# A long-convolution and MLP kernel: two filter blocks transformed whole, a wide-matmul FIR, DMA transposes for five MLP inputs, folded inverses, a new order

## The chip, the cores and the metric

The kernel runs on one core of a Trainium2 chip. TensorE multiplies matrices and writes to PSUM, VectorE and ScalarE do element-wise work, GpSimd computes the small powers of the norms and issues accumulating DMAs, and SyncE issues the other DMAs. The metric is the device time in microseconds (us); a time without a label is the median of several runs. Times inside a profile are those of one profiled execution, counted from the start of its span.

## The reference, cut to what matters

The input is one sequence of 2048 positions with 512 channels in bf16. It passes twice through two layers:

```python
x = A_q
x = x + A(layernorm(x), A_k, A_v, shift_k, ssm_k, ssm_D)
x = x + B(layernorm(x), w1, b1, w2, b2)
x = x + A(layernorm(x), A_k, A_v, shift_k, ssm_k, ssm_D)
x = x + B(layernorm(x), w1, b1, w2, b2)
```

Layer A shifts k with a causal FIR filter of four taps per channel (`shift_k`), multiplies by v to get kv, convolves kv along the positions with a causal filter as long as the sequence (`ssm_k`, in the reference by FFT), adds `kv * ssm_D`, and multiplies the result y by its normalised input q. Since k and v do not depend on x, y is the same in both passes. Layer B is an MLP: a second layernorm, a matrix of 512 x 1376, GELU, a matrix of 1376 x 512, and biases.

## The kernel before, in words

**Blocks.** The sequence is cut into four blocks of 512 positions. One buffer `ar` in SBUF holds everything in bf16, `sm` the statistics, `ps` is PSUM. In a block a partition holds four neighbouring positions, so that a tile is 128 x 512 (positions by channels).

**The convolution.** Each block of kv and each block of the filter is transformed to 512 odd frequencies by matmuls with a table of cosines and sines (`forward`, line 582, for kv; `spectrum_h`, line 598, for the filter, which first transposes it on TensorE). `forward` uses a symmetry: the even and the odd positions are transformed apart (two matmuls for each of two outputs, four tiles, 16 matmuls of 512 columns a block, in `freq`, line 575), ScalarE evicts each tile out of PSUM, and VectorE makes the sum and the difference, which are the frequencies and their mirror images. Products of spectra of blocks j and b-j are made on VectorE (`products`, line 677), and for j over 0 are added into the accumulator by accumulating DMAs that GpSimd issues (`accumulate`, line 620). `wrap` (line 664) adds the wrapped part of the previous filter block. At the end of `products` VectorE combines real and imaginary parts and the mirrored halves; `inverse` (line 709) turns the result into y, for blocks 1 to 3 with 16 matmuls of 512 columns.

**The FIR.** `shift` (line 622) transposes k on TensorE, evicts it into a layout with one spare column for the previous block's last value, and multiplies by diagonal matrices of the four taps (built by one VectorE instruction, line 570). A half block takes 32 matmuls of 128 columns (line 648); two halves, four blocks, 256 matmuls. VectorE multiplies the result by v (block 0 straight out of PSUM, line 657).

**The MLP.** `mlp(b, L)` (line 784) does layer A's last step and layer B for block b in pass L. For two pairs of 128-position tiles it computes statistics on VectorE or ScalarE, the power on GpSimd (line 738), the last coefficient on VectorE (line 739), the norm on ScalarE (line 779), multiplies by y, adds, and does a second norm the same way. The normalised pair is transposed by eight 128 x 128 transposes on TensorE (line 807) and evicted by ScalarE or VectorE (lines 563 and 564) into the MLP's input. The first matrix follows (line 824; 44 matmuls of 512 columns, or 88 of 256 where `PARTS`, line 860, cuts the block in two), GELU on ScalarE (line 829), the second matrix (line 843; 44 of 512 columns), and VectorE adds the result to x (line 848 in pass 0, with the sum for the next mean; line 851 in pass 1).

**What sets the order.** The program is recorded as a list of operations with their reads and writes. A written-out list (`ORDER`) says in which order each engine takes its operations, `BANKS` which PSUM bank each tile has, and `SIDE` which of those that could run on ScalarE or VectorE take the second choice. Engines work strictly in this order and wait for each other by semaphores; SyncE and GpSimd issue DMAs in their order too. `keep_busy` fills TensorE's longer planned gaps with idle matmuls (line 913; 34 of them here).

**Program order around the change.** H0, block 0's convolution, H1, MLP(0,0), block 1's convolution, H2, H3, the wraps, then MLPs and the convolutions of blocks 2 and 3. The order list interleaves all of it.

Of the kernel before, what the change touches and what calls it, by code (L numbers as in the profile page):

```python
# [366 lines left out]
def _tables():  # L367

    t = np.arange(4)[:, None] + 4 * np.arange(128)[None, :]
    kk = np.arange(2)[:, None] + 2 * np.arange(128)[None, :]  # L370
    th = TWO_PI * t[:, :, None, None] * (kk + 0.5) / 1024
    F = np.stack([np.cos(th), -np.sin(th)], 3)
    return F.transpose(1, 0, 2, 3, 4).reshape(128, 2048), F.transpose(4, 2, 3, 0, 1).reshape(128, 2048) / 512


SIDE = [30, 204, 508, 590, 728, 750, 831, 912, 933]
BANKS = "020402242404224400262556463010456340262616542032024240042240042440066016553462243501654013266102613202040404062341663552015021261526103315215340424444026015654624643030521242141654360010665123404156021610322554431541243501601"
ORDER = [
# [47 lines left out]
def bass_interleave_layers__ssm_conv_h3__mixer_channel_mlp__prompt_kernel(  # L426
# [141 lines left out]
    dg = A(0, 128, R_DG, [128, 16], [1, 128])  # L568
    i3, s3 = A(0, 128, R_ID, [0, 16], [1, 128]), A(0, 128, R_S, [1, 16], [0, 128])
    P.op(DVE, lambda e: e.tensor_tensor(dg, i3, s3, ALU.mult), 2300.0, reads=[i3, s3], writes=[dg])  # L570
# [26 lines left out]

    def spectrum_h(m):
# [10 lines left out]
        if m == 0:  # L609
            tt(A(0, 1, o, [1, U]), A(0, 1, o, [1, U]), A(0, 1, R_D, [1, U]), ALU.add, 512)  # L610
        forward(o, R_H[m], (R_TMP, R_HT[0], R_EO[0], R_EO[0])[m], m > 0)
# [10 lines left out]
    def shift(b):  # L622
        kt = R_KT[b % 2]
        tl = Tile(P, 2)
        ins = [(c, i, A(0, 128, KS(b) + i * U + c * 128, [1, 128])) for c in range(4) for i in range(4)]

        def f(e, ins=ins, tl=tl):
            for c, i, src in ins:
                r = e.transpose(QB(tl, 0, 128, c * U + i * 128, [1, 128]), src, IDN)  # L629
            return r  # L630
        P.op(PE, f, 16 * 60.0, reads=[x[2] for x in ins] + [IDN], tile=tl)
        copy(A(0, 128, kt + 1, [129, 16], [1, 128]), tl, lambda tl=tl: QB(tl, 0, 128, 0, [128, 16], [1, 128]), 2048, (ACT, DVE), True)
        if b:
            d, e0 = A(0, 128, kt, [129, 16]), A(0, 128, R_KT[1 - b % 2] + 128, [129, 16])
            P.op(DVE, lambda e: e.tensor_copy(d, e0), 110.0, reads=[e0], writes=[d])
        for h in range(2):
            tl = Tile(P, 2)
            ins = []
# [237 lines left out]
    spectrum_h(0)  # L876
    conv(0)
    tag("H1")
    spectrum_h(1)
    tag("KP")  # L880
    keep()
    tag("W1")
# [61 lines left out]
```

## Time and profile before

| what | us |
|---|---|
| median of 3 runs | 246.11 (245.12 to 246.13) |
| the profiled execution's own time | 244.91 |
| its span | 243.1 |

The span is what the profile covers; its own time has 1.8 us around it. In the lists of the profile, a row names the line of the kernel, the engine, the operation, the output and input, the tile sizes and the count. `ar<-ps` is a move from PSUM to SBUF. The mean duration of a matmul in those lists is longer than the distance between two of them, since they are pipelined; distances are read from the chain of work that ended last, whose pieces follow one another without overlap. The chain gives a start, a length and a run of instructions for each piece. The table of stretches gives the busy time of each engine in chosen parts of the span.

### The profile page before, as it was taken

Reading aid. Unit: us, or ns where it says so; the run is one execution under the profiler, and the core shown is the slowest. Engines: PE = TensorE matmul, PEld = TensorE weight load, DVE = VectorE, ACT = ScalarE, POOL = GpSimd, SP = SyncE. Lnnn points to the kernel's source line nnn. Section 1 sums busy time; section 2 is a strip of 40 time slices with the busy share of each in tenths; the row PEclk is TensorE's granted clock in tenths of the full one; section 3 lists DMA queues with packets and bytes.
Section 4 is the critical chain, followed back from the end, with each engine's and each line's share of the span. In section 5 each row is a group of like instructions: output and inputs, shape, how many; then the busy total and the mean of one; then the engine's idle time right before and its main releaser. Section 6 shows DMA issues by size and latency. Waiting matters only on the chain.

```text
span 243.1 us, 3962 instructions
## 1 busy us (share of the span) xinstructions
PE 232.9 (96%) x1551; PEld 131.9 (54%) x1574; DVE 185.1 (76%) x357; ACT 181.6 (75%) x279; POOL 68.0 (28%) x73
## 2 busy tenths in 40 slices
PE   8999996989999999999999999999999999999994
PEld 3756632647655684445444544544468654448841
DVE  1379999999999999999999999783977242574004
ACT  2358998999899589979799285579968657955730
POOL 0000134432572356753146315241310201120000
PEclk9999999999999999999999999999999999999999
DMA  6999916668794099990089989920002000002002
GB/s 189 392 377 220 391 52 238 105 242 162 142 158 62 0 173 173 175 174 3 0 162 185 172 215 226 207 47 3 1 0 89 0 0 3 0 0 86 3 0 86
DMA packets 14406, 29.85 MB, mean 123 GB/s; under 512 B 3026, under 2 KB 8500, under 8 KB 14260
## 3 DMA queue, kind: packets, MB, share of 16 engines
q0 software_dynamic: 5232, 15.21, 32.9%
q1 hardware_dynamic: 9156, 14.40, 17.2%
q8 instruction: 12, 0.20, 0.3%
q14 instruction: 6, 0.05, 0.1%
HBM read 12.30 MB, written 2.10 MB: 59 GB/s over the span
## 4 chain that ended last, share of the span: by engine, by line
PE 67%; DVE 22%; issue 5%; ACT 3%; POOL 2%; DVEq 0%; POOLq 0%
PE ps L824 28%; PE ps L843 26%; DVE ar L557 14%; PE ps L575 6%; DVE sm L750 4%; PE ps L913 3%; PE ps L807 2%; POOL sm L738 2%; ACT ar L779 1%; DVE ar L657 1%; ACT ar L563 1%; DVE ar L851 1%; PE ps L629 1%; PE ps L648 1%; DVE sm L752 1%
## 5 line engine op out<-in xcount | busy, mean ns | idle before, releaser
L557 DVE TENSOR_TENSOR ar<-ar 128x2048 bf16<-128x2048 bf16 (+2 forms) x125 | 115.1, 954 | 9.3 <-ACT ar L563 4.8
L824 PE MATMUL ps<-ar 128*128 128x256 bf16 (+3 forms) x479 | 80.2, 320 | 1.2 <-ACT ar L563 0.9
L563 ACT ACTIVATE ar<-ps 128x1024 bf16<-128x1024 f32 (+2 forms) x61 | 64.3, 1115 | 22.0 <-PE ps L575 10.3
L843 PE MATMUL ps<-ar 128*128 128x512 bf16 (+1 forms) x339 | 79.6, 379 | 0.7
L829 ACT ACTIVATE ar<-ps,sm 128x256 bf16<-128x256 f32 (+3 forms) x121 | 61.5, 572 | 16.5 <-PE ps L824 16.2
L738 POOL TENSOR_TENSOR sm<-sm 128x2 f32<-128x2 f32 x32 | 39.0, 1218 | 104.6 <-DVE sm L757 45.1
L824 PEld LDWEIGHTS ps<-ar 128*128 128x128 bf16 (+1 forms) x484 | 47.7, 100 | 32.3 <-ACT ar L563 1.8
L779 ACT ACTIVATE ar<-ar,sm 128x512 bf16<-128x512 bf16 x64 | 48.4, 808 | 13.3 <-DVE sm L739 13.1
L843 PEld LDWEIGHTS ps<-ar 128*128 128x128 bf16 (+1 forms) x352 | 34.1, 98 | 37.0 <-ACT ar L829 1.2
L575 PE MATMUL ps<-ar 128*128 128x512 bf16 x187 | 44.4, 380 | 3.5 <-ACT ar L563 2.7
L620 POOL DMA_DIRECT2D ar<-ar x30 | 27.5, 931 | 44.8 <-DVE ar L557 25.3
L750 DVE BATCH_NORM_STATS2 sm<-ar 128x6 f32<-128x512 bf16 x48 | 32.5, 687 | 0.4
L575 PEld LDWEIGHTS ps<-ar 128*128 128x128 bf16 x192 | 17.2, 98 | 27.2 <-ACT ar L563 7.7
L851 DVE TENSOR_TENSOR ar<-ps,ar 128x512 bf16<-128x512 f32 x16 | 10.9, 686 | 16.6 <-PE ps L843 16.5
L848 DVE SCALAR_TENSOR_TENSOR ar<-ps,ar 128x512 bf16<-128x512 f32 x16 | 11.0, 685 | 8.4 <-PE ps L843 8.3
L648 PE MATMUL ps<-ar 128*128 128x128 bf16 x256 | 15.6, 219 | 0.3 <-ACT ar L563 0.2
L648 PEld LDWEIGHTS ps<-ar 128*128 128x128 bf16 x256 | 14.7, 98 | 1.8 <-ACT ar L563 0.7
L564 DVE COPY ar<-ps 128x1024 bf16<-128x1024 bf16 (+1 forms) x9 | 7.3, 808 | 7.7 <-PE ps L605 3.9
L771 ACT ACTIVATE ar<-ar,sm 128x512 bf16<-128x512 bf16 x16 | 11.5, 717 | 0.1
L913 PE MATMUL ps<-ar 128*128 128x512 bf16 x34 | 9.4, 428 | 1.0 <-DVE ar L523 1.0
L807 PE MATMUL ps<-ar 128*128 128x128 bf16 x128 | 9.5, 219 | 0.5 <-ACT ar L779 0.4
L807 PEld LDWEIGHTS ps<-ar 128*128 128x128 bf16 x128 | 8.1, 98 | 3.0 <-ACT ar L779 0.9
(27 smaller groups left out, 53.5 us busy)
## 6 DMA issues: line engine op xcount, KB each, us to landing
ar<-ar POOLq DMA_DIRECT2D x24, 512.0 KB, 4.9
ar<-in_A_k_dram SPq DMA_DIRECT2D x4, 512.0 KB, 5.6
ar<-in_A_ssm_k_dram SPq DMA_DIRECT2D x4, 512.0 KB, 8.0
ar<-in_A_v_dram SPq DMA_DIRECT2D x4, 512.0 KB, 5.8
ar<-in_A_q_dram SPq DMA_DIRECT2D x4, 512.0 KB, 7.0
ar<-ar POOLq DMA_DIRECT2D x6, 256.0 KB, 4.6
out_dram<-ar SPq DMA_DIRECT2D x3, 512.0 KB, 2.6
ar<-in_B_w_dram SPq DMA_DIRECT2D x1, 1376.0 KB, 7.1
```

The costliest lines, as they stand in the source:

```text
L557: return P.op(DVE, lambda e: e.tensor_tensor(o, a, b, op), 66.0 + 0.52 * n, reads=[a, b], writes=[o])
L563: return e.activation(dst, src(), AF.Copy)
L575: r = e.matmul(Q(tl, 0, 128, ri * 512, [1, 512]), w, m, start=a, stop=z)
L620: P.op(POOL, lambda e: e.dma_start(dst, src, accum_op=ALU.add), 880.0, reads=[src, dst], writes=[dst], dma=True, nbytes=nb)
L648: r = e.matmul(Q(tl, 0, 128, q, [1, 128]), w, m, start=j == 0, stop=j == 3)
L738: P.op(POOL, lambda e: e.tensor_tensor(r, v, hf, ALU.pow), 1100.0, reads=[v, hf], writes=[r])
L750: P.op(DVE, lambda e, st=st, x=x: e.bn_stats(st, x), 600.0, reads=[x], writes=[st])
L779: P.op(ACT, lambda e: e.activation(o, x, AF.Identity, bias=m, scale=r), 705.0, reads=[x, m, r], writes=[o])
L807: r = e.transpose(QB(tl, 0, 128, 256 * j + 128 * a, [1, 128]), src[4 * a + j], IDN)
L824: r = e.matmul(Q(tl, 0, rows, 0, [1, n]), w, m, start=dk == 0, stop=dk == 3)
L829: P.op(ACT, lambda e, dst=dst, tl=tl, rows=rows, bias=bias, n=n: e.activation(dst, Q(tl, 0, rows, 0, [1, n]), AF.Gelu_apprx_tanh, bias=bia ...
L843: r = e.matmul(Q(tl, 0, 128, 0, [1, 512]), ins[fc][0], ins[fc][1], start=fc == 0, stop=fc == 10)
```

## The change

1. **Filter blocks 1 and 2 transformed whole.** A new `direct` replaces `forward` for them: for each of the four outputs all eight matmuls (four positions, real and imaginary) accumulate in one PSUM tile, 32 matmuls a block instead of 16, and the sum and difference on VectorE go. A negated copy of half of the table (`negate`, one instruction, on ScalarE by `SIDE`) supplies the mirrored outputs.
2. **Frequency numbering.** The second half of the frequencies is numbered from the other end (`768 * np.arange(2)`), which makes the two halves mirror images in the time fold; `wrap` treats both halves alike (a subtraction on VectorE, an accumulation by DMA).
3. **FIR in wide matmuls.** For a channel group seven matmuls of 512, 384, 256, 128, 384, 256 and 128 columns replace sixteen of 128; 112 in all instead of 256, over the same number of columns. The diagonals are built in two halves, and block 0's transposes and evictions are cut in two.
4. **Five MLP inputs transposed by DMA.** For MLPs (1,1), (2,0), (2,1), (3,0) and (3,1) SyncE issues four DMA transposes of 128 x 512 each (20 in all, 128 KB each) straight from the normalised tile into the MLP's input; their 80 transposes on TensorE and ten evictions go.
5. **Inverses of blocks 2 and 3 folded once more.** Four more VectorE products of 1024 elements at the end of `products` halve the inverse: 8 matmuls instead of 16.
6. **H2 is recorded ahead of MLP(0,0)**, the power's planned cost falls from 1100 to 690 ns, and `ORDER`, `BANKS` and `SIDE` are new. By the new order the idle matmuls are 28.

```diff
-    kk = np.arange(2)[:, None] + 2 * np.arange(128)[None, :]
+    kk = 768 * np.arange(2)[:, None] + 2 * np.arange(128)[None, :]
...
-SIDE = [30, 204, 508, 590, 728, 750, 831, 912, 933]
+SIDE = [32, 216]
...
+    negf = A(0, 128, R_HT[0] + 4096, [512, 2], [1, 512])
+    posf = A(0, 128, R_F + 512, [1024, 2], [1, 512])
...
+    P.op((ACT, DVE), negate, {ACT: 930.0, DVE: 360.0}, reads=[posf], writes=[negf])
+
+    def direct(src, dst):
+
+        for c in range(2):
+            for z in range(2):
+                tl = Tile(P, 2)
+                ins = []
+                for ri in range(2):
+                    for i in range(4):
+                        w = A(0, 128, R_HT[0] + 4096 + ((i // 2 * 2 + c) * 2 + ri) * 128, [1, 128]) if z and i % 2 else fw(i, c, ri)
+                        ins.append((ri, i == 0, i == 3, w, A(0, 128, src + i * U, [1, U])))
+                freq(tl, ins)
+                copy(A(0, 128, dst + 2 * c * 1024 + z * 1024, [1, 1024]), tl, lambda tl=tl: Q(tl, 0, 128, 0, [1, 1024]), 1024)
...
+        if m in (1, 2):
+            return direct(o, R_H[m])
...
             for z in range(2):
-                i = 2 * h + z
-                for c in range(4):
-                    for j in range(4):
-                        ins.append((z * 512 + c * 128, j, A(0, 128, kt + (c * 4 + (i - j) % 4) * 129 + (i >= j), [1, 128]),
-                                    A(0, 128, R_DG + (c * 4 + j) * 128, [1, 128])))
+                c = 2 * h + z
+                for m in (0, 1, 2, 3, -1, -2, -3):
+                    ins.append((z * 512 + max(m, 0) * 128, A(0, 128, kt + (c * 4 + m % 4) * 129 + (m >= 0), [1, 128]),
+                                A(0, 128, R_DG + (c * 4 + max(-m, 0)) * 128, [1, 128 * (4 - abs(m))]), m == 0, m == -3, 128 * (4 - abs(m))))
...
+        if b in (2, 3):
+            for o in range(2):
+                u = A(0, 128, R_ACC + 512 + 1024 * o, [2048, 2], [1, 512])
+                v = A(0, 128, R_ACC + 4608 + 3072 * o, [-2048 if o else 2048, 2], [1, 512])
+                for z in range(2):
+                    tt(A(0, 128, R_ACC + 4096 * z + 1024 * o, [2048, 2], [1, 512]), u, v, ALU.subtract if z else ALU.add, 1024)
...
+        if b in (2, 3):
+            for h in range(2):
+                ins = []
+                for o in range(2):
+                    for ri in range(2):
+                        z = h if o == 0 else (h if ri == 0 else 1 - h)
+                        ins.append((o, ri == 0, ri == 1, A(0, 128, R_T + ri * 512 + (2 * h + o) * 128, [1, 128]),
+                                    A(0, 128, R_ACC + 4096 * z + 1024 * o + 2048 * ri, [1, 512])))
+                freq(tls[h], ins)
...
+            if (b, L) in ((1, 1), (2, 0), (2, 1), (3, 0), (3, 1)):
+                for a in range(2):
+                    zs, dst = A(0, 128, z + a * 512, [1, 512]), A(0, 128, xt + (i + a) * 128, [512, 4], [1, 128])
+                    P.op(SP, lambda e, zs=zs, dst=dst: e.dma_start_transpose(dst, zs), 1300.0, reads=[zs], writes=[dst], dma=True, nbytes=1 << 17)
+                continue
...
-    tag("H2")
-    spectrum_h(2)
```

More of the change, by code (lines that the diff above doesn't have):

```diff
@@ L373, in _tables @@
     return F.transpose(1, 0, 2, 3, 4).reshape(128, 2048), F.transpose(4, 2, 3, 0, 1).reshape(128, 2048) / 512
-SIDE = [30, 204, 508, 590, 728, 750, 831, 912, 933]
-BANKS = "020402242404224400262556463010456340262616542032024240042240042440066016553462243501654013266102613202040404062341663552015021261526103315215340424444026015654624643030521242141654360010665123404156021610322554431541243501601"
+SIDE = [32, 216]
+BANKS = "424403420422004444020404264035164326466324116564640250020422402022464353124255405143230236501603412450404002022614426015405436534013043510420400402222051636541226433302001253013461455322064141151652033046463460415621"
 ORDER = [
[41 rows of a table removed]
[41 rows of a table added]
 ]
@@ L565, in copy @@
         P.op(engs, f, {ACT: 70.0 + .833 * n, DVE: 75.0 + n * (.52 if fast else 1.04)}, writes=[dst], tile=tl)
-    dg = A(0, 128, R_DG, [128, 16], [1, 128])
-    i3, s3 = A(0, 128, R_ID, [0, 16], [1, 128]), A(0, 128, R_S, [1, 16], [0, 128])
-    P.op(DVE, lambda e: e.tensor_tensor(dg, i3, s3, ALU.mult), 2300.0, reads=[i3, s3], writes=[dg])
+    for z in range(2):
+        dg = A(0, 128, R_DG + 1024 * z, [128, 8], [1, 128])
+        i3, s3 = A(0, 128, R_ID, [0, 8], [1, 128]), A(0, 128, R_S + 8 * z, [1, 8], [0, 128])
+        P.op(DVE, lambda e, dg=dg, i3=i3, s3=s3: e.tensor_tensor(dg, i3, s3, ALU.mult), 1180.0, reads=[i3, s3], writes=[dg])
     def freq(tl, ins):
@@ L596, in forward, with negate @@
                 tt(A(0, 128, dst + z * 1024, [2048, 2], [1, 1024]), e, o, ALU.subtract if z else ALU.add, 2048)
+    negf = A(0, 128, R_HT[0] + 4096, [512, 2], [1, 512])
+    posf = A(0, 128, R_F + 512, [1024, 2], [1, 512])
+    def negate(e):
+        if e is nc.scalar:
+            return e.activation(negf, posf, AF.Copy, scale=-1.0)
+        return e.tensor_scalar(negf, posf, -1.0, None, ALU.mult)
+    P.op((ACT, DVE), negate, {ACT: 930.0, DVE: 360.0}, reads=[posf], writes=[negf])
[10 more added lines that the diff above has]
+                copy(A(0, 128, dst + 2 * c * 1024 + z * 1024, [1, 1024]), tl, lambda tl=tl: Q(tl, 0, 128, 0, [1, 1024]), 1024)
     def spectrum_h(m):
@@ L623, in shift, with f @@
         kt = R_KT[b % 2]
[L624 to L632, printed above, removed]
+        for z in range(2) if b == 0 else ():
+            tl = Tile(P, 1)
+            ins = [(c, i, A(0, 128, KS(b) + i * U + (2 * z + c) * 128, [1, 128])) for c in range(2) for i in range(4)]
+            def f(e, ins=ins, tl=tl):
+                for c, i, src in ins:
+                    r = e.transpose(QB(tl, 0, 128, c * U + i * 128, [1, 128]), src, IDN)
+                return r
+            P.op(PE, f, 8 * 60.0, reads=[x[2] for x in ins] + [IDN], tile=tl)
+            copy(A(0, 128, kt + 8 * 129 * z + 1, [129, 8], [1, 128]), tl, lambda tl=tl: QB(tl, 0, 128, 0, [128, 8], [1, 128]), 1024, (ACT, DVE), True)
+        if b:
+            tl = Tile(P, 2)
+            ins = [(c, i, A(0, 128, KS(b) + i * U + c * 128, [1, 128])) for c in range(4) for i in range(4)]
+            def f(e, ins=ins, tl=tl):
+                for c, i, src in ins:
+                    r = e.transpose(QB(tl, 0, 128, c * U + i * 128, [1, 128]), src, IDN)
+                return r
+            P.op(PE, f, 16 * 60.0, reads=[x[2] for x in ins] + [IDN], tile=tl)
+            copy(A(0, 128, kt + 1, [129, 16], [1, 128]), tl, lambda tl=tl: QB(tl, 0, 128, 0, [128, 16], [1, 128]), 2048, (ACT, DVE), True)
         if b:
@@ L639, in shift @@
             for z in range(2):
-                i = 2 * h + z
-                for c in range(4):
-                    for j in range(4):
-                        ins.append((z * 512 + c * 128, j, A(0, 128, kt + (c * 4 + (i - j) % 4) * 129 + (i >= j), [1, 128]),
-                                    A(0, 128, R_DG + (c * 4 + j) * 128, [1, 128])))
+                c = 2 * h + z
+                for m in (0, 1, 2, 3, -1, -2, -3):
+                    ins.append((z * 512 + max(m, 0) * 128, A(0, 128, kt + (c * 4 + m % 4) * 129 + (m >= 0), [1, 128]),
+                                A(0, 128, R_DG + (c * 4 + max(-m, 0)) * 128, [1, 128 * (4 - abs(m))]), m == 0, m == -3, 128 * (4 - abs(m))))
             def f(e, ins=ins, tl=tl):
-                for q, j, w, m in ins:
-                    r = e.matmul(Q(tl, 0, 128, q, [1, 128]), w, m, start=j == 0, stop=j == 3)
-                return r
-            P.op(PE, f, 32 * 69.0, reads=[x for y in ins for x in y[2:]], tile=tl)
-            v = A(0, 128, R_V[b % 2] + h * 1024, [1, 1024])
-            if b in (1, 2, 3):
-                t = A(0, 128, R_FT + h * 1024, [1, 1024])
-                copy(t, tl, lambda tl=tl: Q(tl, 0, 128, 0, [1, 1024]), 1024)
+                for q, w, d, a, o, n in ins:
+                    r = e.matmul(Q(tl, 0, 128, q, [1, n]), w, d, start=a, stop=o)
+                return r
+            P.op(PE, f, 14 * 4 + 32 * 53.4, reads=[x for y in ins for x in y[1:3]], tile=tl)
+            v = A(0, 128, R_V[b % 2] + 256 * h, [512, 4], [1, 256])
+            src = lambda tl=tl: Q(tl, 0, 128, 0, [128, 4], [512, 2], [1, 128])
+            if b:
+                t = R_FT + 256 * h
+                copy(A(0, 128, t, [512, 4], [128, 2], [1, 128]), tl, src, 1024)
+                t = A(0, 128, t, [512, 4], [1, 256])
                 tt(v, t, v, ALU.mult, 1024)
                 continue
-            P.op(DVE, lambda e, v=v, tl=tl: e.tensor_tensor(v, Q(tl, 0, 128, 0, [1, 1024]), v, ALU.mult), 1140.0,
-                 reads=[v], writes=[v], tile=tl)
+            v = A(0, 128, R_V[0] + 256 * h, [512, 4], [128, 2], [1, 128])
+            P.op(DVE, lambda e, v=v, src=src: e.tensor_tensor(v, src(), v, ALU.mult), 1140.0, reads=[v], writes=[v], tile=tl)
     def keep():
@@ L669, in wrap @@
             pr, pi = [A(0, 128, prev + 2048 * c + 512 * ri, [1024, 2], [1, 512]) for ri in range(2)]
-            if c:
-                accumulate(re, pi, 410000)
-                tt(im, im, pr, ALU.subtract, 1024)
-            else:
-                tt(re, re, pi, ALU.subtract, 1024)
-                accumulate(im, pr, 410000)
+            tt(re, re, pi, ALU.subtract, 1024)
+            accumulate(im, pr, 410000)
     def products(b):
@@ L707, in products @@
                 tt(A(0, 128, acc + 512 + 1024 * o, *d, [2048, 2], [1, 512]), u, v, ALU.subtract if o else ALU.add, 1024 * n)
+        if b in (2, 3):
+            for o in range(2):
+                u = A(0, 128, R_ACC + 512 + 1024 * o, [2048, 2], [1, 512])
+                v = A(0, 128, R_ACC + 4608 + 3072 * o, [-2048 if o else 2048, 2], [1, 512])
+                for z in range(2):
+                    tt(A(0, 128, R_ACC + 4096 * z + 1024 * o, [2048, 2], [1, 512]), u, v, ALU.subtract if z else ALU.add, 1024)
     def inverse(b):
         tls = [Tile(P, 2) for _ in range(2)]
-        for cs in ((0,), (1,)) if b == 0 else ((0, 1),):
+        if b in (2, 3):
[7 more added lines that the diff above has]
+                freq(tls[h], ins)
+        for cs in () if b in (2, 3) else ((0,), (1,)) if b == 0 else ((0, 1),):
             for h in range(2):
@@ L737, in finish @@
         r, nm = M(0, 128, M_RS + 2 * k, [1, 2]), M(0, 128, M_NM + 2 * k, [1, 2])
-        P.op(POOL, lambda e: e.tensor_tensor(r, v, hf, ALU.pow), 1100.0, reads=[v, hf], writes=[r])
+        P.op(POOL, lambda e: e.tensor_tensor(r, v, hf, ALU.pow), 690.0, reads=[v, hf], writes=[r])
         small(lambda e: e.scalar_tensor_tensor(nm, mn, neg, r, ALU.mult, ALU.mult), [mn, r], nm)
@@ L879, in bass_interleave_layers__ssm_conv_h3__mixer_channel_mlp__prompt_kernel @@
     spectrum_h(1)
+    tag("H2")
+    spectrum_h(2)
     tag("KP")
```

82 rows, old and new, of the table ORDER are left out of this document.

## The prediction

> **What bounds the kernel now.** I read the first part of the page, then a table of stretches, then the chain of work that ended last. The page:
>
> ```profile
> span 243.1 us, 3962 instructions
> ...
> PE 232.9 (96%) x1551; PEld 131.9 (54%) x1574; DVE 185.1 (76%) x357; ACT 181.6 (75%) x279; POOL 68.0 (28%) x73
> ```
>
> TensorE is busy 96% of the span, but matmuls overlap, so this does not yet say that it is full. The stretches, cut where the program changes character (columns: stretch, length, busy us of each engine, granted clock, DMA share, GB/s; the last row is a detail):
>
> ```profile
> 5.60:17.40 11.80, 11.41 (x133) 7.99 (x133) 6.59 (x6) 4.77 (x4) 0.00 (x0) 1.00 1.04 386
> 17.40:91.10 73.70, 68.67 (x575) 42.70 (x580) 72.91 (x128) 65.55 (x84) 26.82 (x25) 1.00 0.68 164
> 91.10:240.10 149.00, 148.17 (x832) 79.35 (x846) 104.57 (x222) 110.03 (x192) 40.76 (x43) 1.00 0.38 79
> 240.10:243.10 3.00, 0.00 (x0) 0.00 (x0) 0.69 (x2) 0.00 (x0) 0.00 (x0) 0.95 0.37 131
> 120.00:160.00 40.00, 39.79 (x207) 19.39 (x209) 37.64 (x73) 27.60 (x46) 16.39 (x18) 1.00 0.90 184
> ```
>
> From 17.4 to 91.1 us VectorE is the fuller one (72.91 of 73.70). After that TensorE is. To see whether it has room there, its work is priced from the chain, whose rows show back-to-back runs without the overlap:
>
> ```profile
> 8.74 1.95 PE ps L648 x32
> ...
> 23.25 1.12 DVE ar L557
> ...
> 45.86 0.58 DVE ar L557
> ...
> 69.30 0.45 PE ps L807 x8
> ...
> 85.99 0.61 DVE ar L848 x2
> ...
> 91.11 9.44 PE ps L824 x43
> ...
> 118.73 4.32 PE ps L824 x20
> ...
> 184.09 3.93 PE ps L824 x36
> ```
>
> A 512-column matmul takes 4.32/20 = 0.216 us, one of 256 columns 3.93/36 = 0.109, a 128-column transpose 0.45/8 = 0.056, a small FIR matmul 1.95/32 = 0.061. A VectorE product of 2048 elements takes 1.12 us, one of 1024 takes 0.58. At 91.11 us the MLP of block 1, layer 0 starts (I write M10 for it, M01 for block 0, layer 1). From there the program holds 576 matmuls of 512 columns (440 in five whole MLPs, 88 in the second halves of M30 and M31, 48 in transform 3 and inverses 2 and 3), 176 of 256, and 96 transposes: 124.4 + 19.2 + 5.4 = 149.0 us, exactly the stretch. **TensorE has no room after 91.1 us: work taken from it there comes off the end**, as long as its inputs come in time.
>
> **The change, part by part.** The late stretch first. Inverses 2 and 3 fall from 16 matmuls to 8 each: 16 x 0.216 = 3.5 us less. Five MLPs lose 80 transposes: 80 x 0.056 = 4.5 us less. What stays is 560 x 0.216 + 19.2 + 16 x 0.056 = 141.1 us, 7.9 less.
>
> With the transposes go ten evictions out of PSUM, seven of them on VectorE:
>
> ```profile
> L564 DVE COPY ar<-ps 128x1024 bf16<-128x1024 bf16 x7 | 4.8, 689 | 3.4 <-PE ps L807 3.4
> ```
>
> The six that stay are all on ScalarE. Against these 4.8 us stand eight more products of 1024 for the folds, 4.6 us, in two groups ahead of inverses 2 and 3. I cost both at nothing at the end, as TensorE covers them; where they decide when an input is ready, they are counted below.
>
> The front. Filter blocks 1 and 2 take 32 matmuls each instead of 16: 32 x 0.216 = 6.9 us more TensorE; four products of 2048 go, 4.5 us of VectorE. The FIR keeps its columns in 112 matmuls instead of 256: a group of seven costs 0.216 + 2 x (0.162 + 0.109 + 0.056) = 0.87 (0.162 for 384 columns lies between the rows), so sixteen groups 13.9 instead of 15.6. Front work goes from 74.8 us (188 wide, 88 half, 256 FIR, 160 transposes) to 80.0. Between 5.6 and 91.1 us 10.7 us hold no real work, 19 idle matmuls (4.1) among them. So M10 starts between 5.6 + 80.0 = 85.6 us (no wait at all) and 91.1 + 5.2 = 96.3 (nothing of the added work hidden).
>
> VectorE says where. In the new order it has, up to M10's last coefficient, 29 products of 2048, 34 of 1024 and 16 statistics, as before, because products of block 2 move up into the room of the four that go; only one accumulation of an MLP output (0.61) is fewer. The very start shortens too:
>
> ```profile
> 5.39 2.29 DVE L570 TENSOR_TENSOR ar<-ar 128x2048 bf16<-128x2048 bf16 x1 [4.47 <-DMA ar<-in_A_shift_k_dram]
> ...
> 6.72 1.88 ACT L563 ACTIVATE ar<-ps 128x2048 bf16<-128x2048 bf16 x1 [4.71 <-PE ps L629]
> ```
>
> Diagonals and first eviction are halved, so the FIR can start after 5.8 + 0.45 + 0.94 = 7.2 us instead of 8.74; seven idle matmuls (1.5 us) in front of it hold it to 7.6: 1.1 us gained. By VectorE M10 comes 0.6 + 1.1 = 1.7 us earlier, at 89.4; with TensorE fuller I take **90.0**. The negation is new on ScalarE, about 1 us by the 1.88 row's half, beside TensorE's FIR.
>
> The twenty crossbar transposes have no row here. Each moves 128 KB from SBUF to SBUF. The nearest rows, with the microseconds from issue to landing:
>
> ```profile
> ar<-ar POOLq DMA_DIRECT2D x24, 512.0 KB, 4.9
> ...
> out_dram<-ar SPq DMA_DIRECT2D x3, 512.0 KB, 2.6
> ...
> out_dram<-ar SPq DMA_DIRECT2D x4, 128.0 KB, 1.7
> ```
>
> and for what an issue holds SyncE (ns, least, median, most), a load of 2-byte pieces:
>
> ```profile
> L495 SPq DMA_DIRECT2D ar<-in_B_b_dram x3: 288/911/3580, 16.0 to 17.3; - x3
> ```
>
> Landing lies between 1.7 us (same size) and 4.9 (four times the size, read, added and written); I take 3.0, nearer the same size, with a wait behind other packets. The pitch at which one follows the other on SyncE's queue lies between 0.3 and 4.9 (one at a time); I take 1.2, near the 0.9 median. Queued behind them on SyncE are the store of block 0 and the load of the last q (behind M20's four), then M11's four behind that load; later the stores of blocks 1 and 2, which nobody reads.
>
> M20 is the tight place, being first. Before:
>
> ```profile
> 130.36 3.64 ACT L779 ACTIVATE ar<-ar,sm 128x512 bf16<-128x512 bf16 x5
> ...
> 134.55 1.06 PE L807 MATMUL ps<-ar 128*128 128x128 bf16 x16
> ```
>
> Its norms ended at 134.0, just ahead of the transposes. In the new order its last coefficient has six products of 2048 and an eviction fewer in front of it and three products of 1024 more: 6.7 + 0.6 - 1.7 = 5.6 us earlier, with the start 6.7, so its norms end at 127.3, and those of the pair ahead two norms (of 3.64/5 each) before that, at 125.8. Four transposes from 125.8 at a pitch of 1.2, plus 3.0, land at 132.4. TensorE wants them at 90.0 + M10 19.0 + transform 3.5 + transposes 0.9 + inverse 1.7 + M01 19.0 = 134.1. No stall, 1.7 us to spare.
>
> Inverse 3 is the other place; the last accumulation and what follows it before:
>
> ```profile
> 155.34 0.84 POOL L620 DMA_DIRECT2D ar<-ar  x1 [1.76 <-DMA ar<-ar]
> ...
> 160.33 2.35 DVE L557 TENSOR_TENSOR ar<-ar 128x2048 bf16<-128x2048 bf16 x2
> ```
>
> 155.3 + 4.9 = 160.2: VectorE waited for the DMA, whose share is 0.90 between 120 and 160 us. Twelve accumulations there take about 3.3 us each, so M20's and M11's eight transposes of a quarter of the bytes add about 6.6. The new order puts block 3's first products about 8 us of VectorE work earlier, which pays for most. TensorE reaches inverse 3 at 134.1 + 19.0 + 7.8 = 160.9; the combining and folding now takes 6.8 us after the accumulations instead of 4.5. I allow **2.0 us** of stall.
>
> Sum: 90.0 + 141.1 + 2.0 + the 3.0 us tail (unchanged last output) = 236.1 us of span. The profiled execution took 244.91, 1.8 more than its span: 237.9; the median of runs is 1.2 above it: **239.1 us**, 2.8% faster.
>
> **Rivals.**
>
> A, DMA collision: the eight transposes delay block 3's accumulations and the earlier start does not pay. They end at 166.8, folding at 173.6, and TensorE stalls 12.7 instead of 2.0: 249.8; half of it gives 244.5. For it: the 0.90, and in that window a 512 KB store needed more than the 2.6 above:
>
> ```profile
> out_dram<-ar SPq DMA_DIRECT2D x1, 512.0 KB, 4.6
> ```
>
> Against it: the queue has 8 us of head start. The Trainium skill (DMA: Bandwidth & Descriptors, "Issuing engines are not separate DMA queues") says that DMAs from SyncE and GpSimd run on the same 16 engines and interleave; the trace agrees (4.6 against 2.6).
>
> B, the front does not hide the added matmuls: M10 at 96.3, 245.4 us. For it: 93% of the front is already TensorE-busy. Against it: M10 waited for VectorE before, and 10.7 us hold no work.
>
> C, the other side: a crossbar transpose occupies its queue until it lands. With 4.9 us each M20's four land at 145.4, a stall of 11.3 that swallows the 2.0 at inverse 3: 248.4 us, or more, since M11 and M30 may wait as well. It decides from 4.3 us each, where M20's stall of 8.9, less the 2.0, eats the 7.0 us of span gained. Against it: the same bytes land on SyncE's queue in 1.7. The Trainium skill (VectorE: DVE Perf Modes, "The three transpose paths") gives a 128x128 bf16 tile 390 ns on TensorE and 1309 ns through the crossbar, and prefers TensorE where PSUM will do; an estimate of four tiles is 5.2 us a transposition, beyond the 4.3. For TensorE the trace differs (56 ns a tile); the crossbar no row shows.
>
> **How the numbers follow.** Forecast 0.60; A 0.13 (0.04 faster, 0.04 same, 0.05 slower); B 0.09 (0.04 faster, 0.05 same); C 0.18, slower. Half a percent, 1.2 us, is about what a measurement tells from no change. So faster 0.68, same 0.09, slower 0.23. The range runs from 235.5 (M10 at 88.4, no stall at inverse 3) to 250.0, up to C with a little more waiting, and A's worst.
>
> **What would show it.** M10's first matmul near 90; the late stretch at 141 us plus stalls; a wait of TensorE for ScalarE or VectorE ahead of inverse 3, of about 2; no wait of L878 for a DMA. Transposes landing after 4.3 us, one after another, mean C; M10 after 94 means B; accumulations landing after 6 us mean A.

## The result, and the profile after

The changed kernel takes **251.36 us** (median of six runs, 250.63 to 251.73) against 245.62 for the kernel before in the same session: ratio 1.023, 95% interval 1.020 to 1.026. It is slower by 5.7 us; the forecast was 239.1, faster, and the time lies above the range. The late stretch lost 9.8 us in one place. The page of the changed kernel:

```profile
span 249.9 us, 3559 instructions
...
PE 233.9 (94%) x1335; PEld 124.5 (50%) x1360; DVE 180.9 (72%) x355; ACT 179.3 (72%) x278; POOL 62.2 (25%) x73
...
PEclk9999999999999999999999858999999999999999
```

TensorE is busy as long as before (233.9 against 232.9) with 216 recorded instructions less, and its granted clock, in tenths in 40 slices of the span, shows 8, 5 and 8 in three of them. Before:

```profile
PEclk9999999999999999999999999999999999999999
```

The table of stretches, cut there (columns as in the prediction):

```profile
17.40:93.70 76.30, 73.13 (x499) 42.62 (x509) 72.52 (x128) 66.28 (x85) 28.20 (x27) 1.00 0.71 172
93.70:139.40 45.70, 44.67 (x215) 20.07 (x216) 44.94 (x92) 41.06 (x67) 19.07 (x21) 1.00 0.65 115
139.40:146.10 6.70, 0.00 (x1) 0.00 (x0) 6.67 (x11) 0.00 (x0) 0.87 (x2) 0.68 1.04 209
146.10:152.00 5.90, 5.88 (x14) 2.30 (x15) 4.52 (x11) 1.26 (x2) 3.15 (x4) 0.50 1.07 251
152.00:246.90 94.90, 94.26 (x513) 50.94 (x521) 45.26 (x109) 64.58 (x121) 10.42 (x14) 1.00 0.24 55
```

M10 starts at 93.7 (before 91.1, forecast 90.0). Then comes a stretch of 6.7 us in which TensorE does nothing while the DMA engines are full (1.04), then 5.9 us at a clock of 0.50. TensorE's timeline (start, length, line, count, and in brackets the idle time ahead of the row and what ended it) says what it waited for, and the chain what the clock cost:

```profile
129.73 9.68 PE L897 MATMUL ps<-ar 128*128 128x512 bf16 x43
146.12 10.11 PE L878 MATMUL ps<-ar 128*128 128x512 bf16 x31 [6.72 <-DMA ar<-ar]
```

```profile
137.76 8.32 DMA ar<-ar
...
146.12 7.42 PE ps L878 x20
...
153.60 4.36 PE ps L878 x19
```

The wait ends with a DMA of `ar` to `ar`: the fourth of M20's transposes, issued at 137.76 and landed at 146.08. Twenty matmuls then take 7.42 us, where the next 20, of which the trace holds 19, take 4.36: 3.1 us lost after the wait itself. M20's last norm was done long before. ScalarE's timeline, then SyncE's (start, length, line, count; norms are L828):

```profile
132.66 0.81 ACT L828 ACTIVATE ar<-ar,sm 128x512 bf16<-128x512 bf16 x1
133.37 0.67 ACT L883 ACTIVATE ar<-ps,sm 96x512 bf16<-96x512 f32 x1
133.94 2.22 ACT L828 ACTIVATE ar<-ar,sm 128x512 bf16<-128x512 bf16 x3
```

```profile
130.80 9.91 SPq L853 DMA_TRANSPOSE ar<-ar  x4
140.76 1.38 SPq L495 DMA_DIRECT2D out_dram<-ar  x1
```

By ScalarE's order M20's last norm is the first of the three at 133.94, of 2.22 / 3 = 0.74 us each, so it is done near 134.7. From there to the landing are 11.4 us. The four issues fill SyncE for 9.9 us, about 2.5 each, so that the fourth, whose norm is done near 134.7, is issued only at 137.76. All twenty (issue in ns, least, median, most; then landing in us):

```profile
L853 SPq DMA_TRANSPOSE ar<-ar x20: 1188/1266/3397, 130.8 to 228.4; - x20
...
DMA to landing us min/median/max: 2.4/2.5/8.3
```

Most land after 2.5 us at a pitch of 1.27, as forecast (3.0 and 1.2). M20's four do not. In that window (128 to 147 us) before and after:

```profile
ar<-ar POOLq DMA_DIRECT2D x6, 512.0 KB, 4.9
```

```profile
ar<-ar POOLq DMA_DIRECT2D x6, 512.0 KB, 7.3
out_dram<-ar SPq DMA_DIRECT2D x1, 512.0 KB, 6.5
ar<-ar SPq DMA_TRANSPOSE x4, 7.2
```

Both land later: block 3's accumulating DMAs after 7.3 us instead of 4.9, M20's transposes after 7.2 instead of the 2.5 of most. Whether they delay each other is what the experiments ask.

The span came out 13.8 us over the forecast sum of 236.1: M10 3.7, the wait 6.7, the half clock 3.1, less the 2.0 allowed at inverse 3 (it waited for nothing), and 2.3 more spread over the late stretch.

### The profile page after: what moved, and what is told of

It is laid out like the page before. It is cut to its first block, busy times and chain, and to the rows that moved or that the text cites. A ratio compares the mean times of both kernels' runs of the same rounds, so it can differ in the third digit from the quotient of the medians.

```text
span 249.9 us, 3559 instructions
## 1 busy us (share of the span) xinstructions
PE 233.9 (94%) x1335; PEld 124.5 (50%) x1360; DVE 180.9 (72%) x355; ACT 179.3 (72%) x278; POOL 62.2 (25%) x73
## 4 chain that ended last, share of the span: by engine, by line
PE 47%; DVE 38%; DMA 6%; POOL 4%; issue 2%; ACT 2%; DVEq 0%; POOLq 0%
DVE ar L557 28%; PE ps L878 20%; PE ps L897 19%; DMA ar<-ar 6%; DVE sm L799 6%; POOL sm L787 4%; PE ps L967 3%; PE ps L577 2%; DVE ar L902 1%; PE ps L684 1%; ACT ar L563 1%; DVE sm L801 1%; ACT ar L828 1%; DVE ar L905 1%; DVE sm L788 0%
## 5 line engine op out<-in xcount | busy, mean ns | idle before, releaser
L878 PE MATMUL ps<-ar 128*128 128x256 bf16 (+3 forms) x479 | 83.3, 328 | 8.3 <-DMA ar<-ar 6.7
L563 ACT ACTIVATE ar<-ps 128x1024 bf16<-128x1024 f32 (+2 forms) x59 | 61.5, 1101 | 19.1 <-PE ps L656 7.7
L787 POOL TENSOR_TENSOR sm<-sm 128x2 f32<-128x2 f32 x32 | 32.4, 1012 | 104.6 <-DVE sm L806 43.9
L828 ACT ACTIVATE ar<-ar,sm 128x512 bf16<-128x512 bf16 x64 | 49.2, 810 | 7.2 <-DVE sm L788 7.0
L577 PE MATMUL ps<-ar 128*128 128x512 bf16 x203 | 47.6, 379 | 0.8 <-ACT ar L563 0.4
L577 PEld LDWEIGHTS ps<-ar 128*128 128x128 bf16 x208 | 19.5, 98 | 23.8 <-ACT ar L563 1.6
L902 DVE SCALAR_TENSOR_TENSOR ar<-ps,ar 128x512 bf16<-128x512 f32 x16 | 11.0, 686 | 16.5 <-PE ps L897 16.5
L820 ACT ACTIVATE ar<-ar,sm 128x512 bf16<-128x512 bf16 x16 | 11.5, 720 | 4.7 <-DVE sm L816 4.6
L684 PE MATMUL ps<-ar 128*128 128x256 bf16 (+3 forms) x107 | 14.2, 283 | 0.7 <-ACT ar L563 0.5
L684 PEld LDWEIGHTS ps<-ar 128*128 128x128 bf16 x112 | 9.6, 98 | 5.0 <-ACT ar L563 0.4
L967 PE MATMUL ps<-ar 128*128 128x512 bf16 x28 | 9.0, 471 | 1.0 <-DVE ar L523 1.0
L788 DVE SCALAR_TENSOR_TENSOR sm<-sm 128x2 f32<-128x2 f32 x32 | 4.8, 154 | 6.1 <-POOL sm L787 6.1
L801 DVE BATCH_NORM_AGGREGATE sm<-sm 128x2 f32<-128x6 f32 x48 | 8.0, 175 | 0.4
L564 DVE COPY ar<-ps 128x2048 bf16<-128x2048 bf16 x2 | 2.5, 1225 | 7.4 <-PE ps L629 4.3
```

Source lines behind the costliest of these rows:

```text
L563: return e.activation(dst, src(), AF.Copy)
L577: r = e.matmul(Q(tl, 0, 128, ri * 512, [1, 512]), w, m, start=a, stop=z)
L684: r = e.matmul(Q(tl, 0, 128, q, [1, n]), w, d, start=a, stop=o)
L787: P.op(POOL, lambda e: e.tensor_tensor(r, v, hf, ALU.pow), 690.0, reads=[v, hf], writes=[r])
L828: P.op(ACT, lambda e: e.activation(o, x, AF.Identity, bias=m, scale=r), 705.0, reads=[x, m, r], writes=[o])
L878: r = e.matmul(Q(tl, 0, rows, 0, [1, n]), w, m, start=dk == 0, stop=dk == 3)
```

## The experiments

**Theory 1**: M20's DMA transposes come late because they share the DMA engines with block 3's accumulating DMAs; TensorE idles and afterwards runs at half clock. **Theory 2**: the front and the folds on VectorE make the loss. Ratios are to the kernel before; the experiments are called e1 to e13. In those that bring transposes back to TensorE (e1, e2, e5 and all built on e5), these and their evictions on ScalarE get places in the order list and PSUM banks; VectorE's order stays as it was.

**M20 on TensorE (e1).**

```diff
-            if (b, L) in ((1, 1), (2, 0), (2, 1), (3, 0), (3, 1)):
+            if (b, L) in ((1, 1), (2, 1), (3, 0), (3, 1)):
```

> Edit: in the changed kernel the input of MLP (2,0), M20, is transposed on TensorE again (16 transposes, two evictions on ScalarE); the other four MLPs keep their DMA transposes. Theory 1 (M20's four DMA transposes come late, TensorE idles 6.7 us and then runs at half clock, about 3.7 us lost): the stall falls under 1 us, the clock stays at 1.00, the transposes cost 16 x 0.056 = 0.9: 251.4 - 6.7 - 3.7 + 0.9 = 241.9 (240.5 to 244). Theory 2 (the front and the folds on VectorE make the loss, and TensorE would wait there or at the next MLP anyway): 249 to 252. In between: MLP (1,1), next in line with the same kind of transposes, takes over part of the wait, 243 to 248.

Measured 250.21 us, ratio 1.016 (1.011 to 1.020). M20 starts without a wait; its successor M11, the next with transposes beside accumulations, takes it over:

```profile
140.43 8.89 PE L878 MATMUL ps<-ar 128*128 128x512 bf16 x40
...
164.90 9.96 PE L878 MATMUL ps<-ar 128*128 128x512 bf16 x36 [4.88 <-DMA ar<-ar]
```

Forty matmuls take 8.89 us at the full clock, 36 take 9.96 after the wait. A miss for theory 1's number: 250.21 lies above even the case in between and within theory 2's 249 to 252. By itself this run decides nothing between the two; the wait for a DMA at M11 says that theory 1 had been applied to one of two places, and e2 and e5 put that to the proof. The six accumulations between 128 and 147 us now land after 5.1 us instead of 7.3: M20's transposes had delayed them as well.

**All five on TensorE (e2).** The condition and the loop of DMAs under it are taken out.

```diff
-            if (b, L) in ((1, 1), (2, 0), (2, 1), (3, 0), (3, 1)):
...
-                continue
```

> Edit: in the changed kernel all five MLP inputs are transposed on TensorE again (80 transposes, ten evictions on ScalarE), the rest of the change is kept. Theory 1: without the stall and the half clock, with 80 x 0.056 = 4.5 us of transposes, 251.4 - 10.4 + 4.5 = 245.5 (244 to 247), 3.6 more than with M20 alone on TensorE. If the four later DMA transpositions cost TensorE as much in waits as they save in transposes, no more than with M20 alone on TensorE. Theory 2: 253 to 256.

Measured 246.21 us, 1.003 (1.001 to 1.005): theory 1's number within 0.7. The clock is 1.00 throughout. Theory 2's least, 253, is 7 us too high: without the DMA transposes the rest of the change leaves the time where it was.

**Idle matmuls in the wait (e3).**

```diff
+    P.fill(lambda e: e.matmul(idle, zero, zeros, start=True, stop=True), 631, 24, cleared)
     P.sync()
```

(631 is M20's first group of matmuls; `fill` puts 24 idle ones ahead of it.)

> Edit: in the changed kernel 24 idle matmuls of 512 columns (24 x 0.216 = 5.2 us) run on TensorE between the last matmul of MLP (0,1) and the first of M20, inside the stall of 6.7 us. Theory 1, its part on the clock: the granted clock stays near 1.00 and M20's first 20 matmuls take 4.3 us instead of 7.4, in all about 3.7 less: 247.7 (246.5 to 248.5); the stall itself stays. If the slow first matmuls of M20 come from something else than the idle time: 251.4, no change.

Measured 249.02 us, 1.012 (1.009 to 1.015):

```profile
139.67 5.34 PE L982 MATMUL ps<-ar 128*128 128x512 bf16 x24
146.49 8.90 PE L892 MATMUL ps<-ar 128*128 128x512 bf16 x40 [1.48 <-DMA ar<-ar]
```

M20 starts no earlier, but its first forty take 8.90 us, as at the full clock in e1. So the half clock came from the idle time and is worth 2.3 us at the end (251.36 less 249.02), less than the 3.7 expected.

**Without block 3's accumulations (e4)**; its sums then lack the products with blocks 1 to 3 of the input.

```diff
-                    if j:
+                    if j and b < 3:
                         accumulate(A(0, 128, a, [1, 2048]), A(0, 128, o, [1, 2048]))
```

> Edit: in the changed kernel the twelve accumulating DMAs of block 3's products are left out (block 3's output then lacks the products with blocks 1 to 3 of the input), all else stays. Theory 1 with contention (M20's transposes land after 4.3 to 8.3 us because they share the DMA engines with these accumulations, and are issued only every 2 to 3 us): they land after about 2.5 us and are issued every 1.3, the stall before M20 falls under 1 us, the time to about 251.4 - 10.4 = 241.0 (239.5 to 243.5). If a DMA transposition is late by itself (queue held until landing, or norms too late): landing 6 us and more, a stall of 5 us and more, 249 to 251.5.

Measured 241.41 us, 0.981 (0.977 to 0.985). SyncE's timeline, M20's first matmuls, and the landing of all twenty transposes:

```profile
130.69 5.20 SPq L853 DMA_TRANSPOSE ar<-ar  x4
```

```profile
139.13 8.88 PE L878 MATMUL ps<-ar 128*128 128x512 bf16 x40
```

```profile
DMA to landing us min/median/max: 2.4/2.5/3.1
```

```profile
93.61:236.80 143.19, 142.46 (x755) 72.54 (x752) 101.08 (x220) 106.81 (x190) 23.82 (x28) 1.00 0.22 50
```

Pitch 1.3, landing at most 3.1, no wait, full clock (the last row, from M10 to the last matmul). The orders of VectorE, ScalarE and SyncE and the start of M20's transposes (130.69, before the edit 130.80) are unchanged, so it is the accumulations beside them that made the transposes late.

**M20 and M11 on TensorE (e5)**, the other three by DMA.

```diff
-            if (b, L) in ((1, 1), (2, 0), (2, 1), (3, 0), (3, 1)):
+            if (b, L) in ((2, 1), (3, 0), (3, 1)):
```

> Edit: in the changed kernel the inputs of M20 and of MLP (1,1), M11, are transposed on TensorE (32 transposes, four evictions on ScalarE); M30, M21 and M31 keep their DMA transposes, which fall after the last accumulation of block 3. Theory 1 (DMA transposes are late only beside the accumulations): no stall of TensorE, the clock stays at 1.00, and against the kernel with all five on TensorE, 246.2, 48 transposes of 0.056 are saved: 243.5 (242.5 to 245). If the later transposes make TensorE wait as well: 246 or more.

Measured **243.25 us, 0.990 (0.987 to 0.993)**: within the expected 242.5 to 245, 1.0% faster than the kernel before and 3.2% faster than the changed one. Its twelve transposes:

```profile
L853 SPq DMA_TRANSPOSE ar<-ar x12: 1189/1259/1277, 175.9 to 219.4; - x12
...
DMA to landing us min/median/max: 2.4/2.5/2.5
```

They begin at 175.9, after the last accumulation, and nobody waits for them. DMA transposes gain 3.0 us where the DMA engines are free (246.21 less 243.25; 48 transposes of 0.056 are 2.7).

**Accumulations in smaller pieces (e6).**

```diff
+                    if j and b == 3:
+                        accumulate(A(0, 128, a + 1536, [-512, 4], [1, 512]), A(0, 128, o + 1536, [-512, 4], [1, 512]))
```

> Edit: in the changed kernel the accumulating DMAs of block 3 move each row of 2048 elements as four pieces of 512 (the same bytes, written from the last piece to the first so that they aren't joined); all else stays, the five DMA transpositions too. A DMA transposition is 544 packets under 512 B, 34 on each of 16 engines; an accumulation's packet is 4 KB and takes about 0.3 us. If the engines alternate between the queues packet by packet, a transposition waits about 34 x 0.3 us at worst, and with packets of a quarter of the size it lands after 3 to 5 us: the stall before M20 falls to 1 to 3 us, without the half clock the time is 243 to 247. If they share by bytes or the queue is slow for another reason: landing 7 to 8 us as before, 250 to 252. If the smaller pieces make the accumulations themselves much slower, TensorE waits at inverse 3, above 252.

Measured 255.61 us, 1.043 (1.038 to 1.048). Packets of the accumulations' queue and landing, 120 to 160 us, first the changed kernel, then this one:

```profile
q0 software_dynamic: 1651, 6.04, 80.4%
...
ar<-ar POOLq DMA_DIRECT2D x12, 512.0 KB, 6.2
...
ar<-ar SPq DMA_TRANSPOSE x5, 6.5
```

```profile
q0 software_dynamic: 5277, 5.24, 91.3%
...
ar<-ar POOLq DMA_DIRECT2D x11, 512.0 KB, 7.7
...
ar<-ar SPq DMA_TRANSPOSE x5, 7.3
```

Of 40 us on 16 engines a large packet took 0.804 x 640 / 1651 = 0.31 us, a small one 0.913 x 640 / 5277 = 0.11; four of them are 0.44. The accumulations became slower and the transposes did not come sooner; TensorE waits 7.95 us ahead of M20 and 2.37 ahead of M11. The time lies in the expectation's third range, above 252, but without its wait at inverse 3. My picture of queues that alternate packet by packet, so that small packets help, is not borne out.

**Plain copies in place of the accumulations (e12)** (block 3's sums are not made; `plain` drops `accum_op` from the DMA).

```diff
-                        accumulate(A(0, 128, a, [1, 2048]), A(0, 128, o, [1, 2048]))
+                        accumulate(A(0, 128, a, [1, 2048]), A(0, 128, o, [1, 2048]), plain=b == 3)
```

> Edit: in the changed kernel (all five MLPs by DMA transposes) the twelve accumulating DMAs of block 3 become plain copies of the same 512 KB, so the sums aren't made; issues and waits stay. If it is the adding that makes the transposes late: landing near 2.5 to 4 us, a stall before M20 under 1.5 us, 241 to 244. If any large transfer on the other queue does it: landing 6 to 8 us, a stall of 5 to 7 us with the half clock, 249 to 252.

Two runs, 242.11 and 246.78 us, too few for a ratio; what follows was read from the profile of the second alone. M20 no longer waits, M11 does. The same window, and TensorE's timeline:

```profile
q0 software_dynamic: 1723, 6.28, 44.0%
...
ar<-ar POOLq DMA_DIRECT2D x12, 512.0 KB, 3.4
...
ar<-ar SPq DMA_TRANSPOSE x8, 4.6
```

```profile
161.75 9.63 PE L878 MATMUL ps<-ar 128*128 128x512 bf16 x35 [2.34 <-DMA ar<-ar]
```

A copy's packet takes 0.440 x 640 / 1723 = 0.16 us, half of an accumulation's. The two rows of transposes, x5 and x8, don't hold the same ones, so they are compared apart: M20's four land after 4.0 us (at most 4.7) beside copies and 7.2 (8.3) beside accumulations; M11's four after 6.2 (7.6) here and 6.4 (7.9) beside accumulations in e1. So plain transfers of this size delay transposes too, and the result lies between my two cases. That the adding makes it worse shows at M20 only, in one execution.

**The front: what makes M10 late?** All on e5. Four edits leave work out: two of four positions of the filter transformation (e7), four of block 2's products (e8), the first plus four of block 1's products (e9), the latter alone (e10). One drops idle matmuls (e11), one moves a product (e13). The first two changed lines are e7's, the next e8's, then e9's and e10's, then e11's:

```diff
-                    for i in range(4):
+                    for i in (0, 3):
...
+                    if (b, c) == (2, 0) and j:
+                        pass
...
+                    if (b, c) == (1, 0):
+                        pass
...
+    P.no_idle_after(15)
```

e13 changes only the order list: the product is taken behind the next addition of an MLP output (L902). M00 is the first MLP.

> Edit: the kernel with M20 and M11 on TensorE, and in the direct transformation of filter blocks 1 and 2 every second pair of matmuls is left out (32 instead of 64, the spectra of both blocks lack two of four positions): 6.9 us less for TensorE ahead of M10, nothing less for VectorE. If VectorE and what it waits for bound the front: M10 still starts at 93 to 94.3 and the time is within 0.7 of the kernel without this edit. If the added matmuls bound the front (B): M10 starts 4 us or more earlier, the time falls by as much.

> Edit: the kernel with M20 and M11 on TensorE, and four VectorE products of 2048 of block 2 (first half of the frequencies, with the kv blocks 1 and 2) are left out, three of them ahead of M10's last coefficient and the fourth right behind it; their accumulating DMAs stay and add old values. If VectorE bounds the front: M10 starts 3 to 4.5 us earlier, at 89.3 to 91, and the time falls by 2.5 to 4.5. If TensorE bounds it (B): M10 at 93 to 94.3, the time within 0.7 of the kernel without this edit.

> Edit: the kernel with M20 and M11 on TensorE; the 32 matmuls of the filter transformation are left out as before (6.9 us less TensorE), and also the four VectorE products of 2048 of block 1's first half of the frequencies (4.5 us less VectorE ahead of the first MLP, M00; old values stand in their place). The first MLP's first matmul is at 59.1 us with either the TensorE work alone or later VectorE products left out. If both engines are at their limit ahead of M00, so that what one saves the other holds back: M00 starts 1.5 to 4 us earlier, at 55 to 57.5, M10 with it, and the time falls by 1 to 4 from 244.5. If something third (the loads, ScalarE, the power on GpSimd) holds the front: no change, M00 within 0.5 of 59.1.

> Edit: the kernel with M20 and M11 on TensorE, and only the four VectorE products of block 1 of the run before are left out, all matmuls stay. If both engines are at their limit ahead of M00: TensorE holds it, M00 within 0.7 of 58.7, the time within 0.8 of 243.3. If VectorE alone bounds the stretch ahead of M00: M00 2 to 4 us earlier and the time too.

> Edit: the kernel with M20 and M11 on TensorE, without the thirteen idle matmuls after the first fifteen (seven ahead of the first FIR, 1.5 us, two behind it, four during M00). The prediction counted 1.1 us for an earlier start of the FIR, of which 0.4 came (8.31 instead of 8.74), as these seven held it. If TensorE holds the front, the FIR starts at 7.2 to 7.6 and all of the front and the end come 0.5 to 1.3 us earlier: 242.0 to 242.8. If VectorE or the loads hold it: 243.3, no change. A lower clock in the front instead of idle matmuls would show as a time above 243.5.

> Edit: the kernel with M20 and M11 on TensorE, and one VectorE product of 2048 of block 2 moved in VectorE's order behind the next addition of an MLP output, which frees the PSUM bank that M10's first transposes wait for (0.9 us in the trace). If VectorE's own order at the end of the front decides when M10 starts: the wait goes, M10 starts 0.6 to 1.2 us earlier, at 92.5 to 93.2, and the time falls to 242.0 to 242.7. If M10's norms on ScalarE hold it anyway (the next wait, 0.6 us, is for them): M10 within 0.4 of 93.76 and 243.3.

Starts in the profiled executions, and M10 counted from the first FIR, whose own start varies with the loads:

| kernel | us (ratio) | first FIR | M00 | M10 | FIR to M10 |
|---|---|---|---|---|---|
| before | 245.62 | 8.74 | 56.40 | 91.11 | 82.4 |
| changed | 251.36 (1.023) | 8.31 | 58.70 | 93.71 | 85.4 |
| e5 | 243.25 (0.990) | 8.38 | 58.77 | 93.76 | 85.4 |
| e7 TensorE less | 244.53 (0.998) | 8.45 | 59.09 | 94.35 | 85.9 |
| e8 later products less | 243.66 (0.992) | 8.68 | 59.08 | 93.99 | 85.3 |
| e9 both less | 245.03 (0.999) | 8.35 | 58.28 | 94.68 | 86.3 |
| e10 early products less | 242.05 (0.986) | 7.67 | 58.02 | 91.39 | 83.7 |
| e11 no idle matmuls | 243.71 (0.994) | 8.19 | 58.56 | 93.62 | 85.4 |
| e13 product moved | 243.74 (0.993) | 8.08 | 58.46 | 93.36 | 85.3 |

Taking TensorE's added matmuls back (e7) makes nothing earlier, although the planner's idle matmuls took only 19 x 0.216 = 4.1 of the 6.9 us again; so the added matmuls alone don't hold the front, and rival B's mechanism is not borne out. Products left out after M00's start (e8) do nothing, those ahead of it (e10) make M10 1.7 us earlier but not M00 (50.4 us after the first FIR in both); with both left out (e9) the gain is gone, TensorE then waiting 1.5 us for an eviction on ScalarE just after M00's start. In e13 the wait stayed at 0.9: the product moved was the one behind the addition, and it is another that stands ahead of it, so this run does not test what it was made for. Without the idle matmuls (e11) TensorE waits 1.2 us for ScalarE's eviction ahead of the first FIR, which starts at 8.19 against 8.38. Eight of its twelve executions took 242.99 to 243.87 us, as e5; the other four took 244.89 to 245.52 at a mean clock of 0.993, the lower clock that the expectation named.

VectorE's own waits say more: the list of who waited for whom (us in total, times, the longest), up to M10, from 15 us on, before and after:

```profile
DVE ar L557 <- ACT ar L563: 1.1, 1, 1.1
DVE sm L739 <- POOL sm L738: 0.5, 1, 0.5
DVE ar L564 <- PE ps L629: 0.4, 1, 0.4
```

```profile
DVE ar L564 <- PE ps L666: 3.1, 1, 3.1
DVE sm L788 <- POOL sm L787: 1.8, 3, 0.6
DVE ar L557 <- ACT ar L563: 0.7, 1, 0.7
```

That is 5.6 us of waiting instead of 2.0, and VectorE's last coefficient for M10 starts at 89.4 instead of 86.6. The 3.1 is one wait, from 15.5 to 18.6 us, for TensorE's transposes of block 1's k, which VectorE evicts; it stands in every run with the new order, and no run takes it away. It need not be worth 3.1: in e8 and e10 part of VectorE's saved work came back as a wait of 3.0 us for an eviction and of 3.2 for a norm on ScalarE. So VectorE's longer waits account for M10's late start, but that removing them would bring it forward is not shown.

## Why the prediction was wrong, point by point

- **TensorE has no room after M10, what leaves it comes off the end: right.** Without contention (e4) the stretch from M10 to the last matmul is 143.2 us, forecast 141.1 plus stalls, before 149.0. Some 2 us of the 7.9 were not seen; why is open.
- **Landing 3.0, pitch 1.2: the step that failed.** Unloaded, 2.5 and 1.27. But M20's four were issued beside accumulations that held the DMA engines at 0.90, a row the prediction quoted itself, and there they took up to 8.3 and 3.4, so that TensorE waited 6.7 us where the prediction had 1.7 to spare. The neighbour chosen, a small store, was measured on idle engines; the other bound, 4.9, was still too low: with the new traffic beside them even the accumulations took 7.3. The 4.6 against 2.6 of a 512 KB store, which the prediction read as a sign of sharing, is none: without the accumulations (e4) the same store takes 4.6, too.
- **"TensorE wants them at 134.1, 1.7 to spare": both ends moved.** TensorE wanted them at 139.4, since M10 was late and small waits added up; M20's last norm came near 134.7, not 127.3. VectorE's last coefficient for it came at 132.3, where before it came at 131.9: counted between the last coefficients of M10 and M20 the order list has 18 products of 2048 instead of 22, but 14 of 1024 instead of 10, so 5.6 us earlier was miscounted; with one accumulation of an MLP output more, the rows give 4 x 1.12 - 4 x 0.58 - 0.61 = 1.6. The prediction counted up to the pair that came last before; in the new order the other pair's coefficient comes last, two products later. This alone would have cost nothing: with the same norms e4 does not wait.
- **M10 at 90.0: the second step that failed**, by 3.7 us. VectorE's instructions up to M10's last coefficient are those counted, but its waits were taken as unchanged: they are 5.6 us instead of 2.0.
- **The half clock was not in the sum**: 2.3 us at the end, by the run with idle matmuls.
- **Rivals.** A had the mechanism, a collision of transposes and accumulations, but looked for it at inverse 3, where no wait came. C had the place, and its time (248.4 or more) came near by luck: it forecast a stall of 11.3 at M20 from a queue held until landing, but even M20's four were issued 1.4 to 3.4 us apart and landed after 4.3 to 8.3; the stall was 6.7, and the half clock, which C did not have, added 3.1. B's sign (M10 at 93.7, its mark 94) came near, but taking the added matmuls back (e7) changed nothing. Of the signs given, M20's landings beyond 4.3 us pointed to C and the accumulations landing after 6 us (7.3) to A; only e4 tells the two apart.
- **Inverse 3, the folds and the FIR**: no stall at the first, and e2 shows that front and folds together leave the time where it was (1.003). The start gained 0.4 us instead of 1.1, and that is within its scatter: over the runs with this front the first FIR starts between 7.55 and 8.88.

## What to carry to other kernels

Move a transposition to the DMA engines only in stretches where their share is low, and price it from rows taken at the share that the new place has: the same DMA took 2.5 us on idle engines and up to 8.3 beside accumulations. When a wait ahead of TensorE is removed, look at the next user of the same path before summing up. When a new order keeps an engine's instructions, count its waits as well. To the price of a long wait of TensorE add the slow matmuls that follow: 3.1 us after 6.7 here.

## What the runs showed of the hardware

A wait of 2.37 us was enough to halve TensorE's granted clock, and the fall came after work had resumed. Stretches of the kernel with smaller pieces (e6), whose wait ahead of M11 ended at 170.48:

```profile
168.00:170.00 2.00, 0.11 (x1) 0.00 (x0) 2.00 (x7) 0.00 (x0) 0.00 (x0) 1.00 1.16 141
170.00:172.00 2.00, 1.52 (x5) 0.61 (x6) 2.00 (x4) 0.10 (x1) 0.00 (x0) 0.76 0.00 0
172.00:174.00 2.00, 2.00 (x6) 0.76 (x5) 1.97 (x3) 1.99 (x4) 0.00 (x0) 0.50 0.00 0
174.00:176.00 2.00, 2.00 (x9) 0.84 (x8) 1.63 (x4) 1.52 (x3) 0.88 (x1) 0.89 0.00 0
```

The clock is 1.00 during the wait, falls near 171.0 and returns near 174.5. The wait of 2.34 us in e12 was followed by the same fall. The Trainium skill (TensorE: Matmul & The Clock Gate, "Part 1: The HAM clock gate") puts the half rate after at least one idle window of about 3.4 us and the full rate after as long a busy one. The fall to 0.50 and the return agree; that a wait of 2.37 is enough does not, and the measurement decides.

Shorter waits left the clock at 1.00 in all profiled executions; the longest of them is in the kernel before:

```profile
41.91 2.59 PE L575 MATMUL ps<-ar 128*128 128x512 bf16 x11 [1.92 <-ACT ar L563]
```

Where the limit lies between 1.92 and 2.34 us, no run shows. How long the half clock lasts does not follow from the wait alone: by the traces' clock records it lasted 3.41 us after 2.34 and 2.37, 6.83 after 4.88 (e1) and after 7.95 (e6, ahead of M20), and 10.24 after the 6.72 of the changed kernel, always one, two or three times 3.41.
